# Delta-rule attention and a Silu feed-forward on one core: the even chunk's scans placed behind the inversion's rows, SyncE's loads in one fixed order, and a feed-forward step between the two units' solves

## The chip, the cores and the metric

The kernel runs on one core of one Trainium2 chip. The metric is the device time of a run in microseconds (us). The core's engines each follow their own list of instructions: TensorE (PE) multiplies matrices, VectorE (DVE) and ScalarE (ACT) work on tiles, GpSimd (POOL) helps with elementwise products, and SyncE (SP) issues most of the transfers between the memory and the on-chip buffers. What the instructions wait for is decided by their data and, where the kernel says so, by an order that is put between them by hand.

## What is computed

The reference is a recurrence over 768 positions, for 4 batches and 8 heads of size 40, followed by a feed-forward with Silu over 3072 rows:

```python
for t in range(S):                       # state: (B, H, 40, 40)
    y[:, :, t] = einsum('bhd,bhde->bhe', r[t], state)
    Sa = einsum('bhde,bhe->bhd', state, a[t])
    state = state * w[t] - einsum('bhd,bhe->bhde', Sa, b[t]) \
            + einsum('bhd,bhe->bhde', v[t], k[t])
x = y.transpose(0, 2, 1, 3).reshape(B * S, 320)
h = x @ w_in                             # 320 -> 2048
out = (h * sigmoid(h)) @ w_out           # 2048 -> 320
```

## The kernel before

The positions are cut into 12 chunks of 64. Inside a chunk, the recurrence becomes a triangular system: products of `a`, `b`, `k` scaled by running products of `w` (a scan), the inverse of a triangular matrix, and a solve with it. A *unit* is one chunk of two batches, so each chunk `n` has two units, `u.m` = 0 and 1. The inverses of an even and an odd chunk are found together, row by row, on VectorE. All is woven with the feed-forward of the chunks that are ready, whose steps wait in `queue`; `take(1)` runs one of them.

The scans of a unit, and what follows from them on GpSimd and ScalarE:

```python
def scale():
    u.W = sb.tile([128, Q, C + 1], F32, name="W", bufs=6)
    R = u.w[:, :, 1 : C + 1]
    pin = partial(in_order, line="vector") if u.n < 2 else lambda x: x
    for be in range(2):
        W, w = ...                                              # cut
        pin(nc.vector.tensor_tensor_scan(W, w, one..., 0.0, ALU.mult, ALU.add))
    pin(nc.vector.reciprocal(R, u.W[:, :, 1 : C + 1]))

def keys():                                                     # of pre()
    nc.gpsimd.tensor_tensor(out=u.kb[:, :, 0], in0=u.kb[:, :, 0], in1=R, op=ALU.mult)
    nc.scalar.activation(out=junk, in_=R, func=AF.Square, accum_out=...)
    nc.scalar.activation(out=junk, in_=u.W[:, :, 1 : C + 1], func=AF.Square, accum_out=...)
```

The products `pm` of a unit (`scores`), masked into `sb`, go through the memory (`md`) into `mi`, so that a whole block lies in one partition. A row of the inversion is one product and one sum; then the inverse `XI` is turned and goes through the memory again (`xd`) into `XT`, whose blocks VectorE transposes:

```python
def row(t):
    n = N - 1 - t
    nc.vector.tensor_tensor(out=part, in0=X[L, :, t + 1 : N, t + 1 : N],
                            in1=M[L, :, t, t + 1 : N]..., op=ALU.mult)
    x = nc.vector.tensor_reduce(out=X[L, :, t + 1 : N, t], in_=part, axis=AX.X, op=ALU.add)
    mark["row"] = x.ins

def back():
    nc.scalar.copy(out=mi[L, 0:16], in_=turned[L, 0:16])
    nc.vector.tensor_copy(out=mi[L, 16:32], in_=turned[L, 16:32])
    send(queue, xd[L], mi[L])

def turned():                                                   # of merge()
    for r in range(0, 128, 32 if small(n) else 64):
        c = r % 64
        pin(nc.vector.transpose(out=X[r : r + 32, :, 32 - c : 64 - c], in_=X[r : r + 32, :, c : c + 32]))
```

Two TensorE products, `first` (`pq`) and `second` (`po`), each copied out by ScalarE, complete the inverse `XT` of a chunk. The steps of a unit's chain, each a group of TensorE products with the copies behind them, are: `keys` (`pt`), `right` (`pr`, from `a` and `GV`), `solve` (`pu` and `pw`, with `XT`; copied by ScalarE into `vl` and `vut`), `read` (`pl`, masked into `vl` by VectorE), `write` (`pgy`, the new state in `GV` and the output `yx`) and `turn`. `keyed` is one more masked product (`pm` into `a`). A feed-forward step is either four products `ph` of a 512-wide block with `w_in`, completed by two with a third of it and followed by two Silu into `gts`, or eight products `po` of `gts` with `w_out`.

An order by hand is laid with these helpers; `product` calls `in_order` for every matmul of the last loop, so TensorE's order there is the program's:

```python
def behind(x, ins, kind=mybir.DependencyClass.NoSync):
    tc.add_manual_dep(x.ins, ins.name, info, reason="in order")

def in_order(x, line="moe"):
    if line in issued:
        behind(x, issued[line])
    issued[line] = x.ins

def send(queue, out, in_):
    x = queue.dma_start(out, in_)
    if queue is nc.scalar:
        in_order(x, "scalar")
    elif "sync" in issued:
        in_order(x, "sync")
    return x
```

The last loop, one pass for each even and odd chunk from 4 on; `ask(n)` loads `v`, `vut`, `vl`, `r` of chunk `n` and `a`, `k`, `b` of chunk `n + 2`:

```python
for n in range(4, NN, 2):
    ask(n)
    ...
    scale, scores = parts_of(prepare(n + 2))
    weave(merges[1:2] + keys + merges[2:3] + right + take(1), scale)
    run(solve + scores[0:1] + take(1) + later[0:2] + scores[2:3] + later[2:3] + scores[1:2] + read + scores[3:4])
    run(take(1) + [partial(keyed, u) for u in units[n + 1]] + write + take(1) + turn)
    ask(n + 1)
    ...
    weave(keys + right + take(1) + solve, scale)
    rows = invert(n + 3)
    merges = rows[35:]
    run(scores + rows[0:1])
    fetch, more = moe(n, xs)
    if n + 3 < NN:
        tail = take(1) + [partial(stack, u) for u in units[n + 3]] + read + take(1)
        tail += [partial(keyed, u) for u in units[n + 2]] + write + take(1)
        queue += more
        weave(tail + [partial(fetch, 0)] + turn + take(8), rows[1:36])
    else:
        ...                                                     # cut
run(queue)
```

Where no order is laid by hand, a scheduler at build time chooses which instruction of an engine comes next, so a scan that stands later in the program can be built ahead of rows that stand earlier.

Of the kernel before, what the change touches and what calls it, by code (L numbers as in the profile page):

```python
# [41 lines left out]
def kernel(  # L42
# [15 lines left out]
    nc = tc.nc  # L58
    NM, NN = aT.shape[0] // 2, aT.shape[1]
    B, S = v.shape[0], v.shape[1]  # L60
    D, H, P, Q = 40, 8, 4, 8
# [132 lines left out]
    issued, mark = {}, {}  # L194
# [29 lines left out]
    def staged(n):  # L224
        return n > 3 and n % 2 == 1

    def load(u, what="abk", queue=nc.sync, wait=None):
        B2 = slice(2 * u.m, 2 * u.m + 2)
        if staged(u.n):

            if u.m == 0:
                mark["stage"] = sb.tile([128, NM, Q, C], F32, name="stage", tag="room")
            u.stage = mark["stage"][:, u.m]
            send(queue, u.stage.rearrange("p (b q) t -> p b (q t)", b=2), aT[B2, u.n].rearrange("b p c -> p b c"))
        elif "a" in what:

            u.a = sb.tile([128, 2, Q, C], F32, name="a", bufs=4)
            for j in range(2):
                J = slice(DP * j, DP * j + DP)
                x = send(  # L240
                    queue,
                    u.a[J, j].rearrange("p (b q) t -> p b (q t)", b=2), aT[B2, u.n, J].rearrange("b p c -> p b c")
                )
                if wait is not None:
                    behind(x, wait, mybir.DependencyClass.Sync)
                    wait = None
        if u.kb is None:
            u.kb = sb.tile([128, Q, 2, C], F32, name="kb", bufs=6)
        for n, x in ((1, bT), (0, kT)):
            for be in range(2 if "kb"[n] in what else 0):  # L250
                send(queue, u.kb[:, P * be : P * be + P, n], x[2 * u.m + be, u.n].rearrange("p (q t) -> p q t", q=P))
# [73 lines left out]
    def pre(u, md):  # L325
        def scale():
            u.W = sb.tile([128, Q, C + 1], F32, name="W", bufs=6)
            R = u.w[:, :, 1 : C + 1]
            pin = partial(in_order, line="vector") if u.n < 2 else lambda x: x
            for be in range(2):  # L330
                W, w = (x[:, P * be : P * be + P].rearrange("p q t -> p (q t)") for x in (u.W, u.w))
                pin(nc.vector.tensor_tensor_scan(W, w, one.rearrange("p q t -> p (q t)"), 0.0, ALU.mult, ALU.add))
            pin(nc.vector.reciprocal(R, u.W[:, :, 1 : C + 1]))  # L333
# [9 lines left out]
        def reciprocals():  # L343
            R = u.w[:, :, 1 : C + 1]
            nc.gpsimd.tensor_tensor(out=u.kb[:, :, 1], in0=u.kb[:, :, 1], in1=R, op=ALU.mult)
            keys()
            k = NM * u.n + u.m
            for x in [6, 7] if k == 4 else [k + 3]:
                if x < NM * NN:
                    load_w(units[x // NM][x % NM], ([w0] + early)[(x - 4) % 3])  # L350
# [28 lines left out]
            for x in (4, 5) if u.n == u.m == 1 else ():  # L379
                load_w(units[x // NM][x % NM], ([w0] + early)[(x - 4) % 3])  # L380

        return [scale, scaled, scores, keys] if u.n < 2 else [scale, reciprocals, scaled, scores]

# [51 lines left out]
    def merge(n, xd, queue):  # L437
# [17 lines left out]
        def turned():  # L455
            for r in range(0, 128, 32 if small(n) else 64):
                c = r % 64
                pin(nc.vector.transpose(out=X[r : r + 32, :, 32 - c : 64 - c], in_=X[r : r + 32, :, c : c + 32]))  # L458
            box["qq"] = sb.tile([128, N, 48], F32, name="qq", tag="tmp" if n > 0 else "xt")


# [99 lines left out]
                )  # L561

    def load_r(u):
        u.r = sb.tile([128, Q, C], F32, name="r", bufs=2)
        u.vut = VUT[u.m]

        u.vl = sb.tile([128, Q, 2, D + C], F32, name="vl", bufs=2)
        T = slice(C * u.n, C * u.n + C)
        B2 = slice(2 * u.m, 2 * u.m + 2)
        for be in range(2):  # L570
            send(
                nc.sync,
                u.vl[0:C, P * be : P * be + P, :, 0:D].rearrange("s p j d -> s (p j) d"),
                v[2 * u.m + be, T, :].rearrange("s (h d) -> s h d", d=D),
            )
        for be in range(2):
            send(
                nc.sync, u.vut[:, P * be : P * be + P, 0], vT[2 * u.m + be, u.n].rearrange("p (q t) -> p q t", q=P)
            )
        send(  # L580
            nc.sync, u.r.rearrange("p (b q) t -> p b (q t)", b=2), rT[B2, u.n].rearrange("b p c -> p b c")
        )
# [259 lines left out]
    md, late = {}, {}  # L842
# [6 lines left out]
            md[0] = dr.tile([128, 32, 32], F32, name="md", bufs=2)  # L849
        return [x for u in units[n] for x in pre(u, md[0])]  # L850

    def parts_of(x):

        return [x[i] for i in (0, 1, 4, 5)] if x else [], [x[i] for i in (2, 3, 6, 7)] if x else []

    def invert(n, chunks=2):

        if n >= NN or n % 2 == 0 and chunks == 2:
# [23 lines left out]
    def run(steps):  # L882
        for step in steps:
            step()
# [60 lines left out]
    for u in units[2] + units[3]:  # L945
# [6 lines left out]
    weave(steps[4:], queue[0:4], convert[14:21])  # L952
    del queue[0:4]
    fetch(1)
    ahead = [parts_of(prepare(n)) for n in (2, 3)]
    weave(
        queue[0:8],
        ahead[0][0] + ahead[0][1] + ahead[1][0] + ahead[1][1] + [partial(keyed, u) for u in units[2]] + invert(3),
        convert[21:31],
    )  # L960
    del queue[0:8]
    for n in range(2, 4):
        for u in units[n]:
            load_v(u)
            load_r(u)
        for u in units[n + 2] if n + 2 < NN else []:
            load(u)
        if n % 2 == 0:
            xs = dr.tile([DM, 4 * NM * C], F32, name="xs", bufs=2)
        steps = [x for pair in zip(*[chain(u, xs) for u in units[n]]) for x in pair]  # L970

        now = {2: 4, 3: 5}.get(n, 8)
        scale, scores = parts_of(prepare(n + 2))
        if staged(n + 2) and n + 2 < NN:
            scale, scores = [x for i in range(2) for x in scale[2 * i : 2 * i + 2] + scores[2 * i : 2 * i + 2]], []
            scores = [partial(stack, u) for u in units[n + 2]]
        weave(steps[0:4], queue[0 : now // 4], scale, convert[31:34] if n == 2 else [])
        more = [partial(keyed, u) for u in units[n + 1]] if n + 1 < NN else []
        rows = invert(n + 2)
        corner = rows[35:]  # L980
        weave(
            steps[4:6] + late.pop(n, []) + more + steps[6:],
            queue[now // 4 : now],
            scores + rows[0:36],
            convert[34:] if n == 2 else [],
        )
        del queue[0:now]
        if n % 2 == 1:
            fetch, more = moe(n - 1, xs)
            fetch(0)  # L990
            queue += more

    def ask(n):
        for u in units[n]:
            load_v(u)
            load_r(u)
        for u in units[n + 2] if n + 2 < NN else []:
            load(u)

    def take(n):  # L1000
        x = queue[0:n]
        del queue[0:n]
        return x


    mark["pair"] = True
    merges = corner
    run(take(8))
    for n in range(4, NN, 2):
        ask(n)  # L1010
        xs = dr.tile([DM, 4 * NM * C], F32, name="xs", bufs=2)
        c = [chain(u, xs) for u in units[n]]
        keys, right, solve, read, write, turn = ([x[i] for x in c] for i in range(6))
        scale, scores = parts_of(prepare(n + 2))
        later = late.pop(n)
        weave(merges[1:2] + keys + merges[2:3] + right + take(1), scale)
        run(solve + scores[0:1] + take(1) + later[0:2] + scores[2:3] + later[2:3] + scores[1:2] + read + scores[3:4])
        run(take(1) + [partial(keyed, u) for u in units[n + 1]] + write + take(1) + turn)
        ask(n + 1)
        c = [chain(u, xs) for u in units[n + 1]]  # L1020
        keys, right, solve, read, write = ([x[i] for x in c] for i in range(5))
        turn = [x[5] for x in c if len(x) > 5]
        scale, scores = parts_of(prepare(n + 3))
        if n + 3 < NN:
            scale += [scores[0], scores[2]]
            scores = [scores[1], scores[3]]
        weave(keys + right + take(1) + solve, scale)
        rows = invert(n + 3)
        merges = rows[35:]
        run(scores + rows[0:1])  # L1030
        fetch, more = moe(n, xs)
        if n + 3 < NN:
            tail = take(1) + [partial(stack, u) for u in units[n + 3]] + read + take(1)
            tail += [partial(keyed, u) for u in units[n + 2]] + write + take(1)
            queue += more
            weave(tail + [partial(fetch, 0)] + turn + take(8), rows[1:36])
        else:
            run(take(1) + read + take(1) + write + take(1))
            fetch(0)
            queue += more  # L1040
    run(queue)
# [154 lines left out]
```

## Time and profile before

| | before |
|---|---|
| median of 3 runs | 978.17 us (967.28 to 993.38) |
| profiled run | 978.86 us, span 977.0 us |
| mean clock granted to TensorE | 0.882 of full |
| `po` steps of the feed-forward (L811) | 768 matmuls, 228.4 us busy |
| `ph` steps (L799 and L804) | 672 matmuls, 252.1 us busy |
| rows of the inversions (L414 and L421) | 338 instructions, 163.0 us busy |
| reciprocals (L333) | 24, 80.3 us busy, 3346 ns each |
| data moved | 82.99 MB, mean 85 GB/s |

The profile is one execution. Busy time is what an engine spent on instructions; a wait is the idle time of an engine just before an instruction, put down to the event that came last. L264 is the helper through which most matmuls go and L217 the one for transfers, so these are told apart by their tiles (`pq`, `pl`, `GV`), not by their line. A matmul of 32-bit numbers shows as two records, so a step of eight `po` matmuls is x16 in a timeline. The share of an engine over the whole span is a mean over stages with different limits: the stages of the last loop are read one by one below.

### The profile page before, as it was taken

To read this page: it belongs to the slowest core of one execution; us is meant where nothing else is said; L and a number is where in the kernel's file an instruction comes from. 1 tells how busy PE (TensorE), PEld (TensorE's weight loads), DVE (VectorE), ACT (ScalarE), POOL (GpSimd) and SP (SyncE) were. 2 spreads that over 40 slices of the span, in tenths; PEclk is the share of its full clock that TensorE was granted. 3 is DMA by queue.
4 is the path that set the end of the run, shared out by engine and by line. 5 is a ranking of instruction groups with operands and counts; after the bars stand their busy time and mean duration, and the time that the engine had idled before them with its cause. 6 is when DMAs were issued, how large, how long until landed. Compare 5 with 4: busy or idle time off the path is not lost.

```text
span 977.0 us, 25377 instructions
## 1 busy us (share of the span) xinstructions
PE 820.9 (84%) x10914; PEld 583.8 (60%) x10914; DVE 564.9 (58%) x1084; ACT 299.6 (31%) x689; POOL 154.5 (16%) x156
## 2 busy tenths in 40 slices
PE   3046599879889949989898989899989999899996
PEld 3046587657768527846637847637756557666544
DVE  9979989774395971374981375971566921610000
ACT  2236285436223314141224141224141133131120
POOL 7402151102022201040211040301040100001001
PEclk9965779997598988788998789898979998999998
DMA  7864736643254604344314344314423221202001
GB/s 151 179 145 126 176 89 170 149 108 86 58 106 96 161 24 90 68 93 106 94 40 82 75 96 112 88 34 92 88 36 76 67 46 32 53 3 72 1 0 30
DMA packets 240150, 82.99 MB, mean 85 GB/s; under 512 B 207136, under 2 KB 231968, under 8 KB 240032
## 3 DMA queue, kind: packets, MB, share of 16 engines
q1 hardware_dynamic: 219488, 69.96, 32.0%
q10 hardware_dynamic: 20544, 11.34, 4.4%
q8 instruction: 87, 1.43, 0.6%
q14 instruction: 31, 0.25, 0.1%
HBM read 67.11 MB, written 14.16 MB: 83 GB/s over the span
## 4 chain that ended last, share of the span: by engine, by line
PE 49%; DVE 34%; DMA 6%; issue 4%; ACT 4%; SPq 1%; POOL 1%; ACTq 0%; POOLq 0%; DVEq 0%
PE po L811 14%; PE ph L799 10%; DVE tmp L414 7%; DVE XI L421 6%; PE pl L264 5%; DVE w L333 4%; PE pm L264 3%; PE po L264 3%; PE ph L804 2%; DVE GV L747 2%; PE pq L264 2%; PE pu L264 2%; PE pt L264 2%; PE pr L264 2%; DVE GV L751 2%
## 5 line engine op out<-in xcount | busy, mean ns | idle before, releaser
L811 PE MATMUL po<-wo_s,gts 128*128 128x320 f32 x768 | 228.4, 454 | 4.9 <-DVE wo_s L190 3.2
L799 PE MATMUL ph<-xt,wi_s 128*128 128x512 f32 (+1 forms) x448 | 195.2, 581 | 0.8 <-DMA xt<-xs 0.8
L811 PEld LDWEIGHTS po<-wo_s,gts 128*128 128x128 f32 x768 | 149.0, 199 | 72.5 <-issue 12.5
L799 PEld LDWEIGHTS ph<-xt,wi_s 128*128 128x128 f32 x448 | 88.0, 206 | 88.5 <-issue 76.2
L806 ACT ACTIVATE gts<-ph 128x512 f32<-128x512 f32 (+1 forms) x112 | 54.7, 533 | 201.8 <-PE ph L804 197.6
L414 DVE TENSOR_TENSOR tmp<-XI,mi 64x2 f32<-64x2 f32 (+40 forms) x169 | 86.5, 512 | 11.5 <-DMA mi<-md 7.3
L333 DVE RECIPROCAL w<-W 128x512 f32<-128x512 f32 x24 | 80.3, 3346 | 0.9
L708 DVE TENSOR_TENSOR vl<-pl,ml 128x512 f32<-128x512 f32 x48 | 30.9, 685 | 84.4 <-PE pl L264 61.0
L421 DVE TENSOR_REDUCE XI<-tmp 64x2 f32<-64x2 f32 (+40 forms) x169 | 76.5, 452 | 4.6
L264 PE MATMUL pq<-XT,sb 32*32 32x32 f32 (+1 forms) x1280 | 35.9, 212 | 50.5 <-DVE XT L458 40.9
L827 POOL TENSOR_TENSOR ot<-gts,ot 128x320 f32<-128x320 f32 x24 | 23.6, 983 | 335.1 <-ACT gts L825 331.7
L286 DVE TENSOR_TENSOR sb<-pm,ms 128x256 f32<-128x256 f32 x48 | 17.7, 415 | 94.8 <-PE pm L264 94.8
L264 PEld LDWEIGHTS pq<-XT,sb 32*32 32x32 f32 (+1 forms) x1280 | 32.6, 135 | 58.5 <-DVE XT L458 30.2
L358 POOL TENSOR_TENSOR a<-a,W 64x512 f32<-64x512 f32 x32 | 39.3, 1229 | 169.6 <-DMA a<-in_aT 150.4
L264 PE MATMUL pm<-a,kb 64*64 64x64 f32 x1280 | 42.3, 246 | 19.2 <-DMA kb<-in_kT 12.8
L264 PEld LDWEIGHTS pl<-r,vut 64*128 64x128 f32 x768 | 54.6, 222 | 4.8 <-ACT vl L636 2.1
L264 PE MATMUL pl<-r,vut 64*128 64x64 f32 x768 | 55.6, 308 | 2.0 <-ACT vl L636 2.0
L804 PE MATMUL ph<-xt,wl_s 64*128 64x512 f32 (+1 forms) x224 | 56.9, 585 | 0.0
L264 PEld LDWEIGHTS pm<-a,kb 64*64 64x64 f32 x1280 | 38.2, 157 | 25.7 <-POOL kb L361 15.7
L308 DVE TENSOR_TENSOR a<-pm,ml 64x512 f32<-64x512 f32 x48 | 33.1, 689 | 32.3 <-PE pm L264 31.4
L264 PE MATMUL pt<-ident,kb 128*128 128x128 f32 x192 | 32.0, 333 | 22.9 <-DVE a L308 22.5
L1052 DVE TENSOR_SCALAR bad<-pb 1x1 int32<-1x1 f32 x1 | 0.1, 145 | 87.8 <-PE pb L1051 87.8
(108 smaller groups left out, 1081.8 us busy)
## 6 DMA issues: line engine op xcount, KB each, us to landing
kb<-in_bT SPq DMA_DIRECT2D x48, 128.0 KB
vut<-in_vT SPq DMA_DIRECT2D x48, 128.0 KB
r<-in_rT SPq DMA_DIRECT2D x24, 256.0 KB
w<-in_wT SPq DMA_DIRECT2D x45, 128.0 KB
kb<-in_kT SPq DMA_DIRECT2D x44, 128.0 KB
a<-in_aT SPq DMA_DIRECT2D x32, 128.0 KB
vl<-in_v SPq DMA_DIRECT2D x48, 80.0 KB
xs<-yx ACTq DMA_DIRECT2D x48, 80.0 KB
```

The source lines that it names most:

```text
L264: x = what(*x, **y)
L308: x = nc.vector.tensor_tensor(out=u.a[O, j], in0=pm[O].rearrange("p (q t) -> p q t", q=Q), in1=ml[O].unsqueeze(1).to_broadcast([C, Q, C]), ...
L333: pin(nc.vector.reciprocal(R, u.W[:, :, 1 : C + 1]))
L358: nc.gpsimd.tensor_tensor(out=u.a[J, j], in0=u.a[J, j], in1=u.W[J, :, 0:C], op=ALU.mult)
L414: x = nc.vector.tensor_tensor(out=part, in0=X[L, :, t + 1 : N, t + 1 : N], in1=M[L, :, t, t + 1 : N].unsqueeze(2).to_broadcast([hi - lo, I ...
L421: x = nc.vector.tensor_reduce(out=X[L, :, t + 1 : N, t], in_=part, axis=AX.X, op=ALU.add)
L708: nc.vector.tensor_tensor(out=u.vl[:, :, j, D:], in0=pl[j].rearrange("p (q t) -> p q t", q=Q), in1=ml.unsqueeze(1).to_broadcast([128, Q, C ...
L799: in_order(nc.tensor.matmul(ph[n], lhsT=wi_s[:, k, at : at + 128], rhs=xt[:, k, :], start=k == 0, stop=False))
L804: in_order(nc.tensor.matmul(ph[n], lhsT=wl_s[R, i, :], rhs=xt[R, 2, :], start=False, stop=True))
L806: nc.scalar.activation(out=place(2 * i + n)[:, T], in_=ph[n], func=AF.Silu)
L811: in_order(nc.tensor.matmul(po[:, 0:DM], lhsT=place(f)[:, b * 128 : b * 128 + 128], rhs=wo_s[:, NF // 2 * half + f, :], start=f == 0, stop ...
L827: nc.gpsimd.tensor_tensor(out=ot4, in0=rest, in1=ot4, op=ALU.add)
```

## The change

Three things are changed, for the last loop above all. First, the scans and reciprocals of the even chunk are laid behind the last row of the inversion (first unit) and behind the transposes of the even chunk's inverse (second unit), so that VectorE's rows aren't interrupted by them. Second, SyncE's loads of the last loop are all laid in one order, that of the program (`issued["sync"] = mark["mi"]`), and the program names each load's place: `ask` is split into `load_v`, `load`, `load_vut` and `load_vl`. Third, the feed-forward steps of a pass are placed anew, one of them between the two units' solves, and the merge of the odd chunk's inverse is spread over the steps beside them. The work on `k` and the loads of `w` become a step `rest` of their own, behind the scaling of `a`. No arithmetic is added or removed.

```diff
             pin = partial(in_order, line="vector") if u.n < 2 else lambda x: x
+            if "pair" in mark and u.n % 2 == 0:
+
+                pin = lambda x: behind(x, mark["row" if u.m == 0 else "across"])
 ...
         def reciprocals():
             R = u.w[:, :, 1 : C + 1]
             nc.gpsimd.tensor_tensor(out=u.kb[:, :, 1], in0=u.kb[:, :, 1], in1=R, op=ALU.mult)
+
+        def rest():
             keys()
 ...
-        return [scale, scaled, scores, keys] if u.n < 2 else [scale, reciprocals, scaled, scores]
+        return [scale, scaled, scores, keys] if u.n < 2 else [scale, reciprocals, scaled, rest, scores]
 ...
-                pin(nc.vector.transpose(...))
+                x = nc.vector.transpose(...)
+                pin(x)
+                if n % 2 == 0:
+                    mark["across"] = x.ins
 ...
     mark["pair"] = True
+    issued["sync"] = mark["mi"]
+    each(load_v, 4)
+    each(load_r, 4)
+    take(8)
     for n in range(4, NN, 2):
 ...                                     # the even chunk, new
+        run(merges[1:2] + keys + merges[2:3] + right)
+        each(load_v, n + 1)
+        each(load, n + 2, "a")
+        each(load, n + 3)
+        take(1)
+        run(solve[0:1] + later[0:2] + [x[i] for i in (0, 5, 1, 6) if x])
+        take(1)
+        run(solve[1:2] + later[2:3] + [x[i] for i in (2, 7, 3, 8) if x] + read)
+        each(load_vut, n + 1)
+        take(1)
+        run([x[i] for i in (4, 9) if x] + write)
+        each(load_vl, n + 1)
+        each(keyed, n + 1)
+        take(1)
+        x = prepare(n + 3)
+        run([x[i] for i in (0, 2, 5, 7) if x] + turn)
 ...                                     # the odd chunk, new
+        run(keys + [x[i] for i in (1, 6) if x] + right)
+        each(load_v, n + 2)
+        each(load, n + 4, "bk")
+        take(1)
+        run(solve[0:1])
+        take(1)
+        run(solve[1:2] + [x[i] for i in (4, 9) if x])
+        rows = invert(n + 3)
+        merges = rows[35:]
+        run(rows[0:1] + [x[i] for i in (3, 8) if x])
+        take(1)
+        if n + 2 < NN:
+            each(stack, n + 3)
+            x = read + [partial(each, load_vut, n + 2), partial(take, 1)]
+            x += write + [partial(each, load_vl, n + 2)] + [partial(keyed, u) for u in units[n + 2]]
+            fetch, more = moe(n, xs)
+            x += [partial(fetch, 0), partial(queue.extend, more), partial(take, 2)] + turn
+            weave(x + [partial(take, 1)] * 6, rows[1:36])
```

(Here `take(1)` runs a step at once; the lists of the steps that are left out hold the same steps as before, and the two chunks ahead of the loop are woven in a like order.)

## The prediction

> **What bounds the kernel now.** I read the page first: engine shares, then the chain of work that ended last.
>
> ```profile
> PE 820.9 (84%) x10914; PEld 583.8 (60%) x10914; DVE 564.9 (58%) x1084; ACT 299.6 (31%) x689; POOL 154.5 (16%) x156
> PE 49%; DVE 34%; DMA 6%; issue 4%; ACT 4%; SPq 1%; POOL 1%; ACTq 0%; POOLq 0%; DVEq 0%
> ```
>
> TensorE is busy 84% of the span, but the chain runs a third of its time through VectorE: the two alternate. To see where, I cut the span at the first `pq` matmul of each pass of the last loop (TensorE's timeline): 368.00, 515.69, 660.28 and 798.43 us. The passes last 147.7, 144.6 and 138.2 us; the last one, without a new inversion, ends at 879.6 (81.2 us); then come 97 us of feed-forward alone. What TensorE waited for between 368 and 880 us (waits view, that engine and window):
>
> ```profile
> PE pq L264 <- DVE XT L458: 22.6, 6, 13.9
> PE pr L264 <- DMA GV<-in_v: 12.4, 4, 3.1
> PE pt L264 <- DVE yx L756: 4.5, 3, 2.0
> PE pt L264 <- DVE GV L751: 4.3, 3, 1.8
> PE po L264 <- ACT qq L530: 4.3, 8, 0.7
> PE pw L264 <- ACT vut L657: 4.1, 3, 1.4
> ```
>
> That is 52 us (us in total, times, longest). The biggest is the wait for the transposed inverse at the head of a pass. What leads up to it stands in VectorE's timeline of the pass at 515.69 (start, us, then the instruction):
>
> ```profile
> 618.62 0.69 DVE L332 TENSOR_TENSOR_SCAN W<-w,one 128x260 f32<-128x260 f32 x1
> ...
> 620.57 3.35 DVE L333 RECIPROCAL w<-W 128x512 f32<-128x512 f32 x1
> ...
> 625.65 1.45 DVE L414 TENSOR_TENSOR tmp<-XI,mi 128x361 f32<-128x361 f32 x1
> ...
> 628.72 3.33 DVE L333 RECIPROCAL w<-W 128x512 f32<-128x512 f32 x1
> ...
> 652.33 1.16 DVE L421 TENSOR_REDUCE XI<-tmp 128x31 f32<-128x961 f32 x1
> 659.52 0.70 DVE L458 STREAM_TRANSPOSE XT<-XT 32x512 f32<-32x512 f32 x1 [6.04 <-DMA XT<-xd]
> ```
>
> The 31 rows of the inversion (L414, L421) start at 601.1 and end at 653.5 us, 52.4 us. In their midst stand the scans and reciprocals of an even chunk, whose products stand in the next pass: 4 scans and 2 reciprocals, not needed yet. The pass at 660.28 has none of them in its rows, which take 742.24 to 784.0, 41.8 us. So the scans cost the rows 10.6 us. After the rows VectorE idles 6.04 us for the round trip through memory. TensorE in the same pass:
>
> ```profile
> 541.34 7.15 PE L264 MATMUL pl<-r,vut 64*128 64x64 f32 x64
> ...
> 593.65 3.69 PE L264 MATMUL pl<-r,vut 64*128 64x64 f32 x64
> ...
> 652.89 4.57 PE L811 MATMUL po<-wo_s,gts 128*128 128x320 f32 x16
> 660.28 0.24 PE L264 MATMUL pq<-XT,sb 32*32 32x32 f32 x2 [2.82 <-DVE XT L458]
> ```
>
> It ran out of work 2.82 us before the inverse came; ahead of the first pass, 13.87 us before. The first two lines are the same product in the two halves of the pass, 7.15 against 3.69 us: the first ran at about half clock (the stages table grants 0.57 over 540 to 552 us).
>
> **What the Trainium skill says.** *TensorE: Matmul & The Clock Gate*, Part 1 (the HAM clock gate): the clock falls to half after about 3.4 us with little activity and comes back after as long of dense work. The trace agrees: 0.50 granted at 516 to 520 us behind a wait of 3.78, 0.52 at 572 to 576 behind one of 3.05; and 0.57 behind a run of small `pq`/`po` matmuls with short gaps. So a removed wait is worth more than its length. The same page (architectural detail) says ScalarE and VectorE take instructions strictly in order; I rest one rival on it. *DMA: Bandwidth & Descriptors*, anatomy of one DMA, says a transfer's semaphore wait happens on the issuing sequencer before dispatch, so with all loads in one order a load that waits holds up those behind it. The trace before shows one such: SyncE issues `mi<-md` at 597.20, 4 us after the last `md<-sb` at 593.15, and three loads squeezed between.
>
> **The change part by part.** I split a pass in A, from the first `pq` to the end of the odd chunk's scores (`pm<-stage`), and B, from there to the next `pq`; in the pass at 515.69, A is 73.2 us (to 588.93) and B 71.4.
>
> *B, scans behind the rows.* B before: 12.1 us from the scores through `sb`, `md`, `mi` to the first row, 52.4 of rows, 6.8 from the last row to `pq`. After: the rows lose 10.6 and take 41.8. One scan pair with its reciprocal (2 x 0.64 + 3.35 = 4.6 us) falls in the 6.04 us in which VectorE waits for memory, free; the second comes between the even and the odd chunk's transposes and delays only the odd ones, which the new order uses some 13 us later. I add 1 us because both halves of `mi` now load behind the odd scores (before, one half came 40 us ahead), and 1 us for ScalarE (below). B by this chain: 12.1 + 1 + 41.8 + 6.8 + 1 = 62.7. TensorE's own work in B, by the order of the built program and the durations at full clock in this trace (five `ph` steps of 4.7 and five `po` steps of 4.5 are 46.0; `pl` 3.7, `pgy` 5.2, `pm` 1.9, `pt` 2.2): 59 us. So the chain still ends last, by about 4 us, and B is 63 instead of 71.
>
> *A, the step between the solves, and the fixed order of the loads.* The waits in A before: 0.71 + 1.07 (`qq`) + 3.05 (`GV`) + 1.37 (`vut`) = 6.2 us. In the new order a feed-forward step of 4.5 us stands after each unit's solve, over ScalarE's copies of 2.3 us a unit, and the merge product `pq` of the odd chunk is issued a step ahead of the `po` that needs it: the `qq` and `vut` waits go. `GV` is loaded straight behind `right` of the chunk before, 40 us early, instead of last behind `r` and `vl`: the 3.05 go. Half clock in A: `pl` 7.15 for 3.69, `po` 5.64 for 4.57, `ph` 5.85 for 3.70, `pt` 3.11 for 1.97, together 7.8 us more; I expect two thirds to go. One feed-forward step moves from B to A, +4.7. And new: `pw`, `po`, `pl`, `pl` of the second unit follow each other with five PSUM banks (10 bank uses in 6.5 us), +2 for waits on copies. A after: 73.2 - 6.2 - 5.2 + 4.7 + 2 = 68.5; I take 67, since the copies were short in this trace.
>
> Pass: 63 + 67 = 130. The first three passes gain 147.7 - 130 = 18, 144.6 - 130 = 15, and 138.2 - 129 = 9 (the third never had scans in its rows). The rows ahead of the first pass (312.7 to 361.2 us) lose their scans too, and TensorE stood 13.87 us there: 10. The last pass gains the waits (1.07 + 3.08) and some half clock: 5. Sum 57 us. Loads, products and conversions ahead of 310 us are only permuted: 0, give or take 4. The 97 us at the end stay. 978 - 57 = 921, put at **922 us**.
>
> **The rivals.**
> 1. *TensorE becomes the bound, and the gain is a third larger.* If the half clock goes altogether and ScalarE keeps up, A is 62 and B 59 to 62, a pass 122: 25 + 22 + 16 + 11 + 7 = 81 us, or 897. For it: the pass at 660.28 had no half clock at `pl` (3.85). Against: the first and last passes did (6.35, 6.48) in the same order of work, so it isn't one order's doing.
> 2. *ScalarE's order gives the gain back.* In the built program the copy of the inverse, then the square of `w`, then its partner stand among the last three Silu of a pass; the square needs the first reciprocal, 4.7 us after the rows. So the last Silu comes some 7.5 us after the rows, and the last two of eight `po` behind it: `pq` at 8.5 instead of 6.8 after the rows. Two of the three heads with scans have that order, so I count 1 us of the 1.7; if half clock follows the stop of 4 us, 3 more a pass, three passes: 931.
> 3. *SyncE's fixed order stalls.* A load whose buffer is late (`w`, which waits for the last reader of the old one; `vl`, for `write`) holds `md` or `mi`. By the order, every buffer ahead of `md` is free 20 us or more before. A stall of 5 us a pass: 940 to 945.
> 4. *Rows hidden anyway.* If TensorE had had work to fill B, the scans cost nothing: only the waits in A, about 25 us in all: 953. Against it stand the stops at the head of the passes.
>
> **Range and chances.** The terms of 10 + 18 + 15 are tied to one measured number, the 10.6 us; the rest lean on clock and waits. Rivals 1 and 2 set the range: 900 to 946. The runs before spread from 967 to 993, so the median carries some 6 us of its own. Within 2% begins at 958; only rival 4 with a bad spell gets there: 6%. Slower needs a stall of 25 us a pass: 1%.
>
> **What would show it.** Rows of 41 to 43 us in all passes with no scan inside, and the first scan within the 6 us behind them: the B step. Waits of `pq` for `XT` below 12 us, from 22.6, and no wait of `pr` for `GV`: the A step. Passes of 125 to 135 us. A wait of `po` for `gts` at the end of the passes shows rival 2; a long stop of `mi<-md` or `vut` behind another SyncE load, rival 3; unchanged half clock at `pl`, a loss of 3 us a pass. I am wrong if a pass stays above 140.

## The result, and the profile after

The changed kernel takes **901.1 us** (median of 4 runs, 900.4 to 908.0), against 978.0 for the kernel before on the same chip: a ratio of 0.926, 95% interval [0.917, 0.936]. Predicted were 922, with a range of 900 to 946. In a later series it took 899.7 against 978.0, 0.924 [0.916, 0.933].

The page of the changed kernel, engine shares and the chain of work that ended last, in the form shown of before:

```profile
PE 778.9 (87%) x10914; PEld 552.9 (61%) x10914; DVE 557.9 (62%) x1084; ACT 297.4 (33%) x689; POOL 151.4 (17%) x156
PE 45%; DVE 19%; DMA 3%; SPq 2%; issue 1%; ACT 1%; POOL 0%; POOLq 0%; ACTq 0%; DVEq 0%
```

TensorE runs the same 10,914 matmuls and is busy 42 us less: the same work at a higher clock. Its idle time falls by 36 us (from 156.1 to 120.3). So of the 78 us, roughly half is clock and the other half waits. VectorE's part of the chain falls from 34% to 19%.

TensorE's waits, in the window from the first `pq` of the first pass to the end of the last attention (356 to 806 us):

```profile
PE po L825 <- ACT gts L820: 6.7, 3, 3.0
PE pq L264 <- DVE XT L463: 5.6, 4, 3.7
PE pm L264 <- ACT vut L671: 1.3, 3, 0.4
PE pm L264 <- DVE yx L770: 0.5, 1, 0.5
```

Some 14 us are left of 52. The wait for the inverse fell from 22.6 to 5.6, the one for `GV` is gone, as are those for `qq` and for `GV` and `yx` at the heads of the transposes. A new one stands first, of the last feed-forward step for ScalarE's Silu.

VectorE's timeline at the end of the rows, ahead of the pass at 482.14 us:

```profile
471.94 1.16 DVE L419 TENSOR_TENSOR tmp<-XI,mi 128x961 f32<-128x961 f32 x1
473.13 1.16 DVE L426 TENSOR_REDUCE XI<-tmp 128x31 f32<-128x961 f32 x1
474.20 1.28 DVE L335 TENSOR_TENSOR_SCAN W<-w,one 128x260 f32<-128x260 f32 x2
475.58 3.35 DVE L336 RECIPROCAL w<-W 128x512 f32<-128x512 f32 x1
480.21 0.70 DVE L463 STREAM_TRANSPOSE XT<-XT 32x512 f32<-32x512 f32 x1 [1.28 <-DMA XT<-xd]
481.43 0.70 DVE L463 STREAM_TRANSPOSE XT<-XT 32x512 f32<-32x512 f32 x1 [0.51 <-DMA XT<-xd]
482.16 1.29 DVE L335 TENSOR_TENSOR_SCAN W<-w,one 128x260 f32<-128x260 f32 x2
483.58 3.35 DVE L336 RECIPROCAL w<-W 128x512 f32<-128x512 f32 x1
```

The scans and the reciprocal lie in the round trip through memory: the idle time before the first transpose is 1.28 us where it was 6.04. The second pair starts behind the even transposes, while TensorE works on `pq`.

The stretches from one first `pq` to the next (us; busy time of PE, PEld, DVE, ACT, POOL with counts; granted clock, DMA share, GB/s), first of the kernel before:

```profile
368.00:515.70 147.70, 134.55 (x1601) 91.78 (x1601) 86.25 (x151) 40.30 (x89) 24.19 (x22) 0.88 0.36 82
515.70:660.30 144.60, 133.09 (x1601) 91.99 (x1601) 85.81 (x151) 40.33 (x89) 24.56 (x22) 0.89 0.36 81
660.30:798.40 138.10, 128.29 (x1600) 87.12 (x1600) 77.45 (x150) 37.19 (x80) 18.82 (x18) 0.93 0.32 70
```

and of the changed kernel:

```profile
356.00:482.00 126.00, 121.89 (x1600) 83.46 (x1600) 85.70 (x152) 39.43 (x88) 23.41 (x23) 0.97 0.44 97
482.00:606.00 124.00, 120.80 (x1625) 82.11 (x1626) 85.83 (x153) 39.83 (x90) 23.18 (x22) 0.99 0.43 97
606.00:731.00 125.00, 121.84 (x1665) 83.86 (x1659) 81.83 (x152) 40.28 (x90) 20.49 (x20) 0.99 0.37 83
```

Some 122 of 125 us are now filled by TensorE, at 0.97 to 0.99 of full clock. (The windows are round figures; the passes themselves, from `pq` to `pq`, are 126.2, 123.5 and 121.2 us.) TensorE's own work now sets most of a pass. At the end of each one it still stands for what hangs on VectorE's rows, as the two waits on top of the list show. The gain by stage:

| stage | before | after | gain | predicted gain |
|---|---|---|---|---|
| ahead of the rows for the first pass | 312.7 | 310.0 | 2.7 | 0, give or take 4 |
| from there to the first `pq` | 55.3 | 46.0 | 9.3 | 10 |
| pass of chunk 4 | 147.7 | 126.2 | 21.5 | 18 |
| pass of chunk 6 | 144.6 | 123.5 | 21.1 | 15 |
| pass of chunk 8 | 138.2 | 121.2 | 17.0 | 9 |
| last attention | 81.2 | 76.8 | 4.4 | 5 |
| feed-forward at the end | 97.4 | 95.6 | 1.8 | 0 |

### The profile page after: what moved, and what is told of

Read it like the earlier page. It is cut to its first block, busy times and chain, and to the rows that moved or that the text cites. A ratio compares the mean times of both kernels' runs of the same rounds, so it can differ in the third digit from the quotient of the medians.

```text
span 899.2 us, 25358 instructions
## 1 busy us (share of the span) xinstructions
PE 778.9 (87%) x10914; PEld 552.9 (61%) x10914; DVE 557.9 (62%) x1084; ACT 297.4 (33%) x689; POOL 151.4 (17%) x156
## 4 chain that ended last, share of the span: by engine, by line
PE 45%; DVE 19%; DMA 3%; SPq 2%; issue 1%; ACT 1%; POOL 0%; POOLq 0%; ACTq 0%; DVEq 0%
PE po L825 14%; PE ph L813 9%; DVE tmp L419 7%; DVE XI L426 7%; PE pgy L264 4%; PE pl L264 3%; PE ph L818 3%; PE pm L264 2%; SPq L217 2%; PE pt L264 2%; PE pr L264 2%; PE po L264 2%; PE pq L264 2%; PE pu L264 2%; DVE GV L761 1%
## 5 line engine op out<-in xcount | busy, mean ns | idle before, releaser
L825 PE MATMUL po<-wo_s,gts 128*128 128x320 f32 x768 | 224.8, 448 | 17.1 <-ACT gts L820 10.8
L825 PEld LDWEIGHTS po<-wo_s,gts 128*128 128x128 f32 x768 | 145.2, 194 | 82.7 <-ACT gts L820 14.7
L813 PE MATMUL ph<-xt,wi_s 128*128 128x512 f32 (+1 forms) x448 | 182.2, 549 | 2.2 <-ACT ot L834 1.4
L813 PEld LDWEIGHTS ph<-xt,wi_s 128*128 128x128 f32 x448 | 82.1, 192 | 82.3 <-issue 67.9
L841 POOL TENSOR_TENSOR ot<-gts,ot 128x320 f32<-128x320 f32 x24 | 21.8, 907 | 358.1 <-ACT gts L839 352.9
L264 PE MATMUL pq<-XT,sb 32*32 32x32 f32 (+1 forms) x1280 | 34.9, 207 | 32.6 <-DVE XT L463 21.1
L839 ACT COPY gts<-po 128x320 f32<-128x320 f32 x24 | 10.2, 425 | 121.8 <-PE po L825 98.0
L264 PEld LDWEIGHTS pl<-r,vut 64*128 64x128 f32 x768 | 45.4, 189 | 4.7 <-ACT vl L650 2.1
L264 PE MATMUL pl<-r,vut 64*128 64x64 f32 x768 | 46.5, 274 | 2.0 <-ACT vl L650 2.0
L264 PE MATMUL pt<-ident,kb 128*128 128x128 f32 x192 | 29.1, 313 | 21.2 <-DVE a L308 21.2
L348 POOL TENSOR_TENSOR kb<-kb,w 128x512 f32<-128x512 f32 x20 | 24.8, 1238 | 131.9 <-DVE w L336 118.6
```

The source lines that it names most:

```text
L264: x = what(*x, **y)
L813: in_order(nc.tensor.matmul(ph[n], lhsT=wi_s[:, k, at : at + 128], rhs=xt[:, k, :], start=k == 0, stop=False))
L825: in_order(nc.tensor.matmul(po[:, 0:DM], lhsT=place(f)[:, b * 128 : b * 128 + 128], rhs=wo_s[:, NF // 2 * half + f, :], start=f == 0, stop ...
L841: nc.gpsimd.tensor_tensor(out=ot4, in0=rest, in1=ot4, op=ALU.add)
```

## The experiments

Each ran beside the kernel before, which took 978 to 979 us in each series. A and B are the halves of a pass as in the prediction: up to the end of the odd chunk's scores, and from there to the next `pq`.

### Undoing one part at a time

**Scans left to the scheduler.** From the changed kernel:

```diff
-            if "pair" in mark and u.n % 2 == 0:
-                pin = lambda x: behind(x, mark["row" if u.m == 0 else "across"])
```

> The changed kernel with the order of the scans taken back, so that they stand inside the rows of the inversion again (TensorE's order is untouched). If the rows still end the second part of a pass (from the odd chunk's scores to the next merge), the three row blocks with scans grow by 10.6 us each and the time by about 28 us, to 929; the head of the last pass, whose rows never held scans, stays. If TensorE's work now fills that part anyway, less than 8 us: below 909. If the longer stop brings half clock back as well, 12 us on top: 940.

Measured: 939.3 us, 0.962 [0.955, 0.969], 38 us more than with the scans behind the rows, nearest to the third case of the expectation. In the profiled runs (933.2 against 901.1) it is 32. Of these, 27 lie in the three stretches with scans (8.9 us each). Another 7 lie in A of the second and third pass, behind the longer stops. A stays short even so (63 to 64.5); B is 71.9 and 72.0 in the two passes whose rows hold scans and 60.3 in the third, which never had them. TensorE's waits (350 to 860 us):

```profile
PE pq L264 <- DVE XT L460: 45.7, 8, 16.2
```

That is twice what it was in the kernel before (22.6): with the other two parts TensorE is done earlier and stands longer at the same point.

**No fixed order for SyncE's loads**, but the loads still named where the new program has them:

```diff
-    issued["sync"] = mark["mi"]
     each(load_v, 4)
```

> The changed kernel with SyncE's fixed order taken back; the loads keep their new places in the program, and a scheduler orders them. If the place in the program was what mattered (GV is asked for ahead of the step that reads over it), TensorE's wait for GV stays away: 901 to 908. If the fixed order itself did it, the waits of 3 us for GV and the half clock behind them come back in every pass: 920 to 925.

Measured: 906.2 us, 0.926 [0.921, 0.930], 5 us more in the medians, with overlapping intervals. There is no wait for `GV` either. What matters for `GV` is where the program names the load, not that the order is fixed. The wait of `pq` for `XT` is 10.1 us here against 5.6. Whether the fixed order is what saves that is not shown.

**A step behind both solves** instead of between them, in both halves of a pass:

```diff
-        run(solve[0:1] + later[0:2] + [x[i] for i in (0, 5, 1, 6) if x])
-        take(1)
-        run(solve[1:2] + later[2:3] + [x[i] for i in (2, 7, 3, 8) if x] + read)
+        run(solve + [x[i] for i in (0, 5, 1, 6) if x])
+        take(1)
+        run(later[0:3] + [x[i] for i in (2, 7, 3, 8) if x] + read)
 ...                                              # the odd half likewise
```

> The changed kernel with the feed-forward step behind both units' solves instead of between them, in both halves of a pass; the number of steps in each part stays. By waits alone the wait for the copies of qq (1.1 us) and vut (1.4 us) comes back in four passes: 10 us, 911. If the step also keeps the clock up, pl and the po behind it run at half clock again (3.5 and 1.1 us a pass): 18 more, 929. If ScalarE's copies are hidden by now, nothing: 901.

Measured: 926.8 us, 0.944 [0.938, 0.950]. A grows to 72.8, 68.2 and 68.2. TensorE's timeline shows why:

```profile
503.06 4.58 PE L825 MATMUL po<-wo_s,gts 128*128 128x320 f32 x16
507.56 1.20 PE L264 MATMUL pq<-XT,sb 32*32 32x32 f32 x64
509.42 0.24 PE L264 MATMUL po<-XT,qq 32*32 32x32 f32 x2 [0.66 <-ACT qq L538]
510.02 1.38 PE L264 MATMUL po<-XT,qq 32*32 32x32 f32 x62 [0.36 <-ACT qq L538]
511.33 7.09 PE L264 MATMUL pl<-r,vut 64*128 64x64 f32 x64
518.36 5.90 PE L825 MATMUL po<-wo_s,gts 128*128 128x320 f32 x16
```

Two stops of 1.02 us together, for the copy `qq` between the two products of the merge, and then `pl` takes 7.09 us instead of 3.79 and the next step 5.90 instead of 4.57. The stretches of 2 us (columns as above; the clock is the third figure from the right) show the clock over these lines:

```profile
508.00:510.00 2.00, 1.01 (x51) 0.78 (x44) 0.00 (x0) 1.25 (x3) 0.40 (x1) 1.00 1.02 259
510.00:512.00 2.00, 1.98 (x68) 1.91 (x70) 0.00 (x0) 0.62 (x2) 0.00 (x0) 0.71 0.94 213
512.00:514.00 2.00, 2.00 (x24) 2.00 (x22) 0.00 (x0) 0.53 (x1) 0.00 (x0) 0.50 0.57 125
...
520.00:522.00 2.00, 2.00 (x7) 1.30 (x6) 0.00 (x0) 0.00 (x0) 0.00 (x0) 0.73 0.24 53
```

The clock falls within 2 us of the stop and stays at half through `pl` and 2 to 3 us of the dense step behind it, some 10 us, all of them busy. Here a stop of 1 us costs 1 + 3.3 + 1.3 = 5.6 us. In the four even halves the waits for `qq` are 4.1 us, `pl` takes 10.8 us more (6.09, 7.09, 7.09 and 5.66 for 3.79 each) and the four steps 6.7 (7.21, 5.90, 5.91 and 5.97 for 4.57): 21.6. In the odd halves the second solve, with no step ahead of it, waits 5.8 us in three stops for `vl`. Together 27, against 25.6 between the medians.

Those stops in the odd half are longer, and yet cost less (same view, second pass):

```profile
549.60 0.95 PE L264 MATMUL pu<-RHS,XT 64*64 64x40 f32 x25 [1.93 <-ACT vl L650]
...
551.29 3.70 PE L813 MATMUL ph<-xt,wi_s 128*128 128x512 f32 x8
```

A feed-forward step stands 1.7 us behind the stop, and runs at full clock. In two of the three passes the clock doesn't fall at all; in the first it is at half for some 3.4 us only (0.67 over 418 to 420 us, 0.50 to 422, 0.98 to 424). It is the string of small products behind a stop, `pl` above all, that makes it dear.

### Is it the step that keeps the clock, or the missing stop?

In the run just told two things are moved: the step, and the merge product `pq`, which came a step ahead of the `po` that reads its copy. To part them, `pq` is left between the solves and only the step is put behind both, in the even half:

```diff
         run(solve[0:1] + later[0:2] + [x[i] for i in (0, 5, 1, 6) if x])
+        run(solve[1:2])
         take(1)
-        run(solve[1:2] + later[2:3] + [x[i] for i in (2, 7, 3, 8) if x] + read)
+        run(later[2:3] + [x[i] for i in (2, 7, 3, 8) if x] + read)
```

> The changed kernel with one edit in the even half: the merge product (pq) of the odd chunk's inverse is still issued between the two units' solves, but the feed-forward step stands behind both solves. The odd half is as in the changed kernel. Theory one, the step itself keeps the clock up through the string of small products: pl of the first half takes 6 to 7.1 us again, and the time is 915 to 925, near the 926.8 with the step behind both solves in both halves. Rival, the clock falls only because the products stop about 1 us for the merge and its copy qq: with the merge issued early pl stays at 3.8 us and the time is 900 to 906.

Measured: 901.9 us, 0.925 [0.916, 0.934], beside 899.7 for the changed kernel itself. Theory one falls. In TensorE's timeline of this run both solves follow each other directly, as in the run before it, and `pl` stays at 3.79:

```profile
495.80 1.33 PE L264 MATMUL pq<-XT,sb 32*32 32x32 f32 x64
497.06 1.00 PE L264 MATMUL pu<-RHS,XT 64*64 64x40 f32 x27
...
498.44 0.65 PE L264 MATMUL pw<-XT,RHS 64*40 64x64 f32 x30 [0.26 <-ACT qq L538]
499.02 4.57 PE L825 MATMUL po<-wo_s,gts 128*128 128x320 f32 x16
503.53 1.20 PE L264 MATMUL po<-XT,qq 32*32 32x32 f32 x64
504.66 3.79 PE L264 MATMUL pl<-r,vut 64*128 64x64 f32 x64
```

The string of small products is 4.7 us long here (494.3 to 499.0), with one stop of 0.26, and the clock does not fall: `pl` takes 3.79 us in all four even halves. Nor is a string of small products enough by itself: in the changed kernel 8.6 us of `pm` and `pgy` without a stop (511.0 to 519.6) have a granted clock of 1.00. What the change buys in the even half is the distance between `pq` and the reader of its copy; a step between the solves is one way to get it. In the odd half the step stays between the solves in this run, and there it covers the copies `vl`.

The stop makes half clock likely, not certain. The kernel before and the runs with the scans alone, with scans and early loads, and with the step behind both solves have the same two stops in front of `pl`, 0.66 or 0.71 and 0.36 us, in each of their four even halves. In 14 of these 16 `pl` takes 5.6 to 7.2 us. In two it takes 3.85, both in the third pass; here that of the kernel before:

```profile
684.55 0.24 PE L264 MATMUL po<-XT,qq 32*32 32x32 f32 x2 [0.71 <-ACT qq L530]
685.15 1.19 PE L264 MATMUL po<-XT,qq 32*32 32x32 f32 x62 [0.36 <-ACT qq L530]
686.90 3.85 PE L264 MATMUL pl<-r,vut 64*128 64x64 f32 x64
```

Why the clock stayed up in these two is open. With neither stop, in the changed kernel and the runs that keep its early `pq`, `pl` was never above 4.2 us in an even half.

### Adding one part at a time to the kernel before

**Scans behind the rows** (the two lines undone above, and the mark behind the even transposes):

> The kernel before with the scans behind the rows, and nothing else (TensorE's order is untouched). TensorE can win what it waited at the three heads with scans, 13.9, 4.5 and 3.7 us, less what it still waits there: 8 to 10 at the first, 4 at each of the others, some 18 in all, and up to 4 for half clock behind those stops: 957. If the rows alone set the second part of a pass, 10.6 at each head: 946.

Measured: 957.2 us, 0.977 [0.971, 0.982]. The wait of `pq` for `XT` falls from 22.6 to 4.7, yet B is only 69.9, 68.3 and 69.8 where it was 73.7, 71.3 and 69.7: the timeline of TensorE has a feed-forward step right up to `pq`, so its own work there takes over as the bound. B gives only some 7 of the 22 us. Some 9 come from the rows ahead of the first pass (its `pq` starts at 359.3 instead of 368.0). Some 7 come from A of the second and third pass (70.3 for 73.3 and 64.5 for 68.4), whose heads have no stop and so no half clock behind it. The same part gives 22 us here and 38 in the changed kernel.

**The values' loads behind the products before**:

```diff
     def ask(n):
         for u in units[n]:
-            load_v(u)
+            if n == 4:
+                load_v(u)
             load_r(u)
 ...
+        ahead = [partial(load_v, u) for u in units[n + 1]]      # n + 2 in the odd half
-        weave(merges[1:2] + keys + merges[2:3] + right + take(1), scale)
+        weave(merges[1:2] + keys + merges[2:3] + right + ahead + take(1), scale)
```

> The kernel before with the loads of GV asked for straight behind the product right of the chunk before, and nothing else. In the profile before, the last of four pieces a unit waits for turn, whose transposes read over the end of their columns into it. TensorE's four waits for GV, 12.4 us, should go; with the half clock behind them (ph 5.4 to 5.9 for 3.7 us, and pr), 9 us more: 957. By the lengths of the waits alone: 966. If SyncE's order holds GV up all the same: 978.

Measured: 972.3 us, 0.992 [0.987, 0.996], 7 us less, half of what the lengths of the waits alone would give. **Scans and early loads together**:

> The kernel before with both the scans behind the rows and the early loads of GV. If the two gains lie in different parts of a pass, they add: about 936. If the earlier start of the rows only moves the wait to another place, less: 945.

Measured: 946.6 us, 0.966 [0.960, 0.972]; its waits (350 to 850 us) have none for `GV`, but

```profile
PE pu L264 <- ACT vl L642: 10.7, 3, 3.7
```

in its place: three stops of 3.6 us, of the second unit's solve for ScalarE's copies of the first. The load was the last of two things that TensorE waited for, and the other stood right behind.

**A step between the solves**:

```diff
-        run(solve + scores[0:1] + take(1) + later[0:2] + scores[2:3] + later[2:3] + scores[1:2] + read + scores[3:4])
+        run(solve[0:1] + later[0:2] + scores[0:1] + take(1) + scores[2:3] + solve[1:2])
+        run(later[2:3] + scores[1:2] + read + scores[3:4])
 ...
-        weave(keys + right + take(1) + solve, scale)
+        weave(keys + right + take(1) + solve[0:1] + take(1) + solve[1:2], scale)
 ...                                              # one take(1) less in the second part
```

> The kernel before with a feed-forward step between the two units' solves in both halves of a pass, as in the changed kernel; one step moves from the second part of a pass to the first. The waits for qq and vut, 8.4 us in all, go; if half clock at pl and po goes with them, 13 more, but the moved step adds 4.7 us at the two heads where the rows end last: 966. If half clock stays: 979.

Measured: 953.0 us, 0.974 [0.969, 0.979], 13 better than expected: `pl` runs at full clock in all eight halves (3.8 to 4.4 us). Where all of the 13 us come from was not followed. The waits of `pq` for `XT` (22.6) and of `pr` for `GV` (12.0) are as before.

**Step and early loads together**:

> The kernel before with two parts of the change: a step between the solves, and the values' loads behind the products before; the scans are left where they were. Alone they gave 26 us (953.0) and 7 us (972.3). Theory: alone, the early load only moved TensorE's wait from the load to ScalarE's copies, which the step covers, so together they give more than their sum: 930 to 940, with no wait of pr for GV and under 4 us of pu for vl. Rival, the gains only add: 944 to 950.

Measured: 958.0 us, 0.985 [0.975, 0.994]. Both expectations fail: the early loads add nothing to the step and perhaps take something (the intervals overlap). The wait for `GV` is gone, but behind the second half's scores stands this:

```profile
570.15 2.24 PE L264 MATMUL pm<-stage,kb 64*64 64x64 f32 x62 [1.75 <-ACT vl L636]
572.32 7.09 PE L264 MATMUL pl<-r,vut 64*128 64x64 f32 x64
579.34 5.84 PE L799 MATMUL ph<-xt,wi_s 128*128 128x512 f32 x8
```

With the step alone the same three took 0.42 us of stop, 3.79 and 3.70: the 2.6 us of waiting for `GV` had given ScalarE the time it needed. Now a stop of 1.75 with half clock behind it costs some 7 us more. In the first pass the same stop of 1.75 left the clock full (`pl` 3.79).

**All three parts in the old order**:

> The kernel before with all three parts: scans behind the rows, early loads of the values, a step between the solves; the rest of its order stays. Singly they gave 22, 7 and 26 us. If they only add: 922 to 928. If each opens what the others left shut (TensorE has no surplus work left behind the rows, the wait on copies is covered): 904 to 914, near the 906.2 of the changed kernel without the fixed order of loads. If the new places of the other steps and of the work on k carry part of the gain themselves, it stays above 914 with waits that the changed kernel doesn't have.

Measured: 922.3 us, 0.946 [0.937, 0.956], 56 us below the kernel before, about the sum of the single gains (22, 7 and 26), though it is no sum of its pairs (scans with early loads gave 32.5, step with early loads 20; scans with the step alone were not tried). It is 22.6 us above the changed kernel in the same series. TensorE's waits for 350 to 860 us begin with the stop just seen:

```profile
PE pm L264 <- ACT vl L642: 5.2, 3, 1.7
```

In the second pass stop, `pl` (7.09 for 3.69 us) and `ph` (5.95 for 3.70) cost 1.75 + 3.4 + 2.25 = 7.4 us, and `pl` takes 7.09 in all three passes: some 21 us. The first two passes are indeed 7.5 and 6.2 us longer than those of the changed kernel. The third is 13.9 longer: there a second stop, of 0.97 us with no cause in the trace, has half clock behind it in the even half. What makes the copy late is in ScalarE's timeline of the same pass:

```profile
540.71 0.63 ACT L343 ACTIVATE junk<-w 128x512 bf16<-128x512 f32 x1 [5.82 <-DVE w L336]
...
543.04 0.76 ACT L642 ACTIVATE vl<-pu 64x320 f32<-64x320 f32 x2
...
546.78 1.08 ACT L812 ACTIVATE gts<-ph 128x512 f32<-128x512 f32 x2
547.89 0.76 ACT L642 ACTIVATE vl<-pu 64x320 f32<-64x320 f32 x2
```

ScalarE stands 5.82 us before a square whose reciprocal VectorE hasn't made, and the copies behind it come late. The changed kernel's ScalarE is through with these squares before it turns to the copies of the solves (its timeline, same place):

```profile
534.78 0.63 ACT L344 ACTIVATE junk<-W 128x512 bf16<-128x512 f32 x1
...
536.50 0.76 ACT L650 ACTIVATE vl<-pu 64x320 f32<-64x320 f32 x2
```

The steps `rest` and the new places of the odd chunk's scaling are what differs ahead of it; and a feed-forward step stands between the scores and `pl` besides. Which of these saves the time was not tried alone.

### The new wait, and the mark

**The squares of the even chunk behind the last Silu**, and the last five pieces of the inversion behind all steps:

```diff
+            last = (lambda x: behind(x, mark["silu"])) if "pair" in mark and u.n % 2 == 0 else lambda x: x
-            nc.scalar.activation(out=junk, in_=R, func=AF.Square, ...)       # both squares likewise
+            last(nc.scalar.activation(out=junk, in_=R, func=AF.Square, ...))
 ...
-            weave(x + [partial(take, 1)] * 6, rows[1:36])
+            weave(x + [partial(take, 1)] * 6, rows[1:32])
+            run(rows[32:36])
```

> The changed kernel with ScalarE's squares of the even chunk laid behind the last Silu of a pass, so that no Silu waits for a reciprocal behind the rows. The waits of po for gts at the heads of the passes (3.0, 2.2 us) should go and the po behind them run at full clock (4.6 instead of 6.3 us). If that was the end of the chain, 3 to 4 us a head at two heads: 894. If the transposed inverse, which comes 6.6 us after the rows, ends the pass as well, 1.3 us a head: 898.

Measured: 902.9 us, 0.923 [0.919, 0.927]: not told apart from the changed kernel; the expected 898 lies within the spread of its runs (897.6 to 906.1). The wait did not go: in its timeline the last `po` step still waits 2.23 us, since ScalarE's copy of the finished inverse (`mi`) stands ahead of the Silu and waits for the last row. The step then runs at full clock (4.58 us), but `pq` now waits 0.51 and 0.69 us for the inverse: the next bound stands right behind the first.

**The changed kernel once more**, as the mark for the last three of these runs:

> The changed kernel once more, as the mark for the three others on the same chip: 898 to 905 us, passes of 121 to 127 us.

Measured: 899.7 us (898.2 to 903.6); passes of 126.5, 122.0 and 120.9 us.

## Why the prediction held, step by step

The time lies just inside the range, at its lower end: 901 against 922, and nearer to rival 1's 897. The step on VectorE's rows held. The sum for A was too long by 4 to 6 us a pass.

**B was right in sum: 63 predicted, 63.0, 63.0 and 60.3 measured.** In the pass at 356 us the parts are 10.8 us from the scores to the first row (predicted 13.1), 44.3 of rows (41.8), and 7.9 from there to `pq` (7.8). That the first two misses cancel is luck. Of the 2.5 us by which the rows are longer, 1.1 is a wait for the buffer of `yx` in their midst and 1.2 lies in the rows' own instructions, which was not followed. Undoing the scans gives B back its 72 us; that shows the step. In the third pass, whose rows never held scans, B fell as well, from 69.7 to 60.3, mainly by the 4.7 us of the step that moved to A, 3.3 of waits ahead of `pt` and 1.9 of half clock at a `ph` step.

**"B by this chain still ends last, by about 4 us" is right in size, but the chain's end is another.** TensorE's own work was set at 59 us; B's 63.0 less the stop for Silu and the half clock behind it is 58.3. At the ends of the first two passes `pq` does not wait for the inverse at all. What waits is the step ahead of it:

```profile
475.95 6.26 PE L825 MATMUL po<-wo_s,gts 128*128 128x320 f32 x16 [2.96 <-ACT gts L820]
```

The way from the rows leads over ScalarE here: its copy of the inverse waits for the last row, and the Silu stands behind the copy. That is rival 2's way. The way over the inverse itself ends within a microsecond or two of it: in the experiment on the squares the one wait shrank, the other came, and no gain stands out from the spread of the runs.

**A was mis-sized: 67 predicted, 63.2, 60.5 and 60.9 measured.** Two terms of its sum failed. Of the 7.8 us of half clock "two thirds" were to go; nearly all went: `pl` takes 3.79 us in the first, second and last head (4.17 in the third) and the step behind it 4.58. `pt` takes 1.97 in the second and third pass, but 2.97 in the first, behind the stop of 3.68 that is left there. And the 2 us set down for waits on PSUM banks and copies did not come; the only wait for copies left in A is 0.4 us. Without them the sum is 73.2 - 6.2 - 7.8 + 4.7 = 63.9. Of the 3.4 us more that the second pass gained, 2.7 are half clock on products that the 7.8 left out: `pq` 1.0, `pr` 0.9, `pm<-stage` 0.8. A carries some 16 of the 21 us between 922 and 901.

**The reason given for the clock was half right.** The prediction named both the step after each solve and `pq` issued a step ahead. Only the second was needed in the even half. The Trainium skill's *TensorE: Matmul & The Clock Gate*, Part 1 (the HAM clock gate), names an idle window of some 3.4 us as what lowers the clock. Here 1.02 us of stops among small products were enough (the dense step ends at 507.6, the clock falls between 510 and 512), four times in four in that run and 14 in 16 with the others, while 4.7 us of small products with 0.26 us of stop left the clock full. The page's figure for an idle stretch does not cover this, and the measurement decides. The same section says that the window runs free of the program; that would fit the two exceptions and the stops of 1.9 us which lowered the clock once in three times, but no run here shows the window.

**`GV`: the wait went as predicted, its cause was another.** I took the load to come late as the last behind `r` and `vl`. SyncE's timeline of the kernel before shows six of eight pieces issued early:

```profile
527.58 3.88 SPq L217 DMA_DIRECT2D GV<-in_v  x6
...
566.47 0.55 SPq L217 DMA_DIRECT2D GV<-in_v  x1
...
570.89 0.54 SPq L217 DMA_DIRECT2D GV<-in_v  x1
```

One piece of each unit is held until the transposes of the old `GV` are through (`GT<-GV`, 562.4 to 572.7), which read past the half that they turn, into the columns that this piece writes. In the new program the load is named ahead of these transposes, and all eight pieces go out together:

```profile
487.38 6.14 SPq L217 DMA_DIRECT2D GV<-in_v  x8
```

Added alone to the kernel before it gave 7 us, and none on top of the step: behind a wait for a load there stood one for ScalarE.

**The rivals.** Rival 1 came true for the most part: hardly any half clock is left in A, and the passes are near its 122. The argument held against it, that the half clock "isn't one order's doing", was half wrong: the order sets the stop in front of `pl`, and without a stop no even half fell; but with it two even halves in 16 kept their clock, as the one did that the prediction names. Rival 2 is there in small: `po` waits 6.7 us for `gts` in three heads and takes 6.26 us in two of them where 4.57 is its time. Most of that lies in the time in which the inverse is on its way through memory anyway, so it costs about 1.3 us a head (`pq` comes 7.9 us after the rows there, 6.6 where no squares stand in the way). Rivals 3 and 4 did not come: no load holds `md` or `mi`, and the scans alone are worth 22 to 38 us.

## What to carry to other kernels

Look at what stands right behind a stop of TensorE, not at the stop alone: with a string of small products behind it 1 us cost 5.6, with a dense step soon behind it 1.9 us cost no more than themselves in two heads of three. A removed wait is worth what is left until the next one: find that next wait first (a copy on another engine, a buffer), and remove both together; the early loads gave 7 us or nothing, the scans 22 or 38, by what stood beside them. A product whose copy is read back should be issued one dense step ahead of its reader.

## What was not expected of the hardware

At half clock TensorE was busy without a gap through `pl` for 7 us and the clock did not come back; it did 2 to 3 us into the dense step behind it (511 to 521 us in the run with the step behind both solves), and within 1 us of the dense step's start where that step began 2.6 us behind the end of the stop (421.1 us, same run). In these stretches being busy with 64x64 products was not enough to raise the clock, though it was enough to hold it (`pl` at 3.79 us in the changed kernel). And the mean granted clock of a run is no measure of its time: two runs of the changed kernel with 901.1 and 900.4 us had 0.946 and 0.909, so I compared durations of the same matmul, not means.
